# Threshold attention followed by a SwiGLU block: a slot's closing steps issued behind the next slot's masks, a chunk's last sigmoids issued with its last value product, and the first queries loaded in two parts

## The chip, the cores and the metric

The kernel runs on one core of one Trainium2 chip, in one launch. The metric is the device time in microseconds, and the median of several runs stands for it. Before the change three runs took 1599.44, 1601.48 and 1604.86 us, so the median is 1601.48 us. One profiled execution took 1599.08 us; its span, from the first to the last instruction, is 1597.3 us, and all times inside the profile count from the start of that span.

The engines are named as in the profile: PE is TensorE's matrix multiplication and PEld its loading of weights, DVE is VectorE, ACT is ScalarE, POOL is GpSimd, and SP is SyncE, which here only issues transfers. Each engine works through its own queue of instructions in order.

## The reference

Attention over 8 batches and 8 heads, 576 queries and keys, head size 64. A probability counts only where its score comes within `tau` of the largest of its row. The result is then the input of a SwiGLU block with 512 inputs and 1536 hidden columns. Everything is float32.

```python
def _attn_ref(q, k, v, tau):                      # q, k, v: (8, 8, 576, 64), tau = 0.02
    scores = scale * np.matmul(q, k.transpose(0, 1, 3, 2))      # scale = 1 / sqrt(64)
    thresh = np.max(scores, axis=-1, keepdims=True) - tau
    scores = np.where(scores >= thresh, scores, -1000000000.0)
    scores = scores - np.max(scores, axis=-1, keepdims=True)
    attn = np.exp(scores)
    attn = attn / (np.sum(attn, axis=-1, keepdims=True) + 1e-09)
    return np.matmul(attn, v).astype(np.float32)

def _moe_ref(x, w_gate, w_val, w_out):            # x: (4608, 512), d_ff = 1536
    g = x @ w_gate
    silu = g * (1.0 / (1.0 + np.exp(-g)))
    val = x @ w_val
    return (silu * val @ w_out).astype(np.float32)
```

The weights come as float64 and are put together into float32 by the kernel (splitting on ScalarE, joining on VectorE and GpSimd), which takes up the first 225 us or so.

## The kernel before

The work is cut into **segments**: one segment is two heads of one batch. A segment has **slots**, each of which makes the scores of up to 2 x 128 queries. Eight segments of a first kind (`halved` is false) come first; 28 segments of five slots each follow (`halved` is true), and most of the span is theirs. Between the slots, pieces of the SwiGLU block are given to TensorE: `fill(part)` issues such pieces until `part` is used up. A **chunk** (or unit) is 256 rows of the SwiGLU block.

A slot's `scores` is a generator. What stands before each `yield` is issued together, and the loop further down decides what comes in between.

```python
def scores(seg, t):
    ...                                    # scores on TensorE into two PSUM tiles "sc" (a pool of 2)
    if halved:
        for x, tile_ in enumerate(pss):    # L315: maximum of each half row, VectorE
            nc.vector.tensor_reduce(out=mx[:, 2 * x:2 * x + 2, 0], in_=tile_[:, :, 0:SH], axis=AX.X, op=ALU.max, negate=True)
        meet(mx, m, largest)               # L271: halves of a row exchanged between partitions, VectorE
        nc.vector.tensor_reduce(out=nm[:, 0:m], in_=mx[:, 0:m, :], axis=AX.X, op=ALU.min)            # L318
    ...
        nc.scalar.activation(th[:, 0:m], nm[:, 0:m], AF.Identity, bias=cut, scale=-1.0)              # L327 (L330)
    for x in range(m):
        nc.scalar.activation(ps[x], scs[x], AF.Exp, bias=nm[:, x:x + 1])                             # L331
    yield                                                                                            # first
    turn(1)                                # L365: transposes p of earlier slots, VectorE; keeps the last 1
    for x in range(m):                     # L335: the masks; they also sum each half row
        nc.vector.scalar_tensor_tensor(out=ps[x], in0=scs[x], scalar=th[:, x:x + 1], in1=ps[x],
                                       op0=ALU.is_ge, op1=ALU.mult, accum_out=sm[:, x, 0:1])
    tot = stp.tile([P, 4], F32, name="tot")
    if halved:
        yield                                                                                        # second
        meet(sm, m, same)                  # L274: partial sums exchanged, four small copies on ScalarE
        yield                                                                                        # third
        nc.vector.tensor_reduce(out=tot[:, 0:m], in_=sm[:, 0:m, :], axis=AX.X, op=ALU.add)           # L342
    ...
    nc.vector.reciprocal(out=ri[:, 0:m], in_=tot[:, 0:m])                                            # L345
    ...
    for x in range(m):
        if halved and not split and x % 2:
            nc.gpsimd.tensor_scalar(out=ps[x], in0=ps[x], scalar1=ri[:, x:x + 1], ...)               # L350
        else:
            nc.scalar.activation(ps[x], ps[x], AF.Copy, scale=ri[:, x:x + 1])                        # L352
    if halved:
        unturned.append([seg["p"][:, x, :] for x in at])
    ...
    yield                                                                                            # fourth
```

The loop over the slots, cut to the order of issue:

```python
for n, seg in enumerate(segs):
    for x, t in enumerate(seg["tiles"]):
        go = scores(seg, t)
        next(go)                       # scores, maximum, threshold, exponential
        ...                            # value products p v of the segment before, in its second slot (L432)
        split_weights(); ...
        next(go)                       # transposes of an earlier slot, masks
        if more:
            join_weights()
        fill(part)                     # SwiGLU pieces
        next(go)                       # exchange of the sums
        if len(unsig) >= SIG:
            sigmoids()
        fill(part)                     # SwiGLU pieces
        next(go)                       # sum, reciprocal, scaling
        ...
```

The pieces of a chunk: `gate` (L475, matrix 0) ends with a copy of the product by ScalarE (L491), `value` (L475, matrix 1) ends with a multiplication by VectorE (L498), `sigmoids` puts the sigmoid on what has gathered (ScalarE, L509) and multiplies it in (GpSimd, L511), then loads the exponential's table again (L514). The output of most chunks is computed by seven products of half the size in place of eight (`seven`, L584), for which `sigmoids` also makes sums on GpSimd (L522 to L524). `output` (L551) is the plain form, for the first two chunks.

```python
def sigmoids():
    eng = nc.vector if attended else nc.gpsimd
    for hts, gt, own in unsig:
        nc.scalar.activation(gt, gt, AF.Sigmoid)
        for y, (x, ht) in enumerate(own):
            eng.tensor_tensor(out=ht, in0=ht, in1=gt[:, 2 * y:2 * y + 2, :], op=ALU.mult)
    ...

def block():                           # the SwiGLU pieces in order; fill() takes them one by one
    ...
        for f in range(0, NF, GR):
            if f == EARLY:
                yield from late        # outputs of the chunk before
            yield from gate(j, cs, f, hts, gts)
            ...
            yield from value(j, cs, f, hts, gts)
            if not ready and f == NF - 2 * GR:
                sigmoids()
        if unsig:
            sigmoids()
        late = outputs(unit)
```

The start: `load_qk(0)` fetches q (SyncE's queue) and k (ScalarE's queue) in four transfers each, scales q by 0.125 (L241 on ScalarE for the first two segments, L243 on GpSimd afterwards), and `prepare` transposes k, the first 256 columns of q and the other 320 (L759 to L761).

Of the kernel before, what the change touches and what calls it, by code (L numbers as in the profile page):

```python
# [19 lines left out]
def kernel(  # L20
# [202 lines left out]
    def load_qk(i):  # L223
        b, hp_ = divmod(i, NP)
        raws = []

        free = {1: 0, 2: 1}.get(i)
        for name, src, order in (("q", q, "(j r) (e d) -> e r j d"), ("k", k, "(j r) (e d) -> e r j d" if b == 0 else "(r j) (e d) -> e r j d")):
            if free is None:
                raw = ld.tile([P, NJ, G], F32, name=f"{name}raw")  # L230
            else:
                n = 2 * free + len(raws)
                raw = extra[:, n * S:(n + 1) * S].rearrange("p (j d) -> p j d", d=G)
            queue = nc.scalar if i < 2 and name == "k" else nc.sync
            for g in range(NG):
                h, e = divmod(g, 2)
                queue.dma_start(out=raw[g * G:(g + 1) * G],
                                  in_=src[b, 2 * hp_ + h].rearrange(order, r=G, d=G)[e])
            raws.append(raw.rearrange("p j d -> p (j d)"))
        if i < 2:  # L240
            nc.scalar.activation(raws[0], raws[0], AF.Copy, scale=scl)  # L241
        else:
            nc.gpsimd.tensor_scalar(out=raws[0], in0=raws[0], scalar1=scl, scalar2=None, op0=ALU.mult)  # L243
        return raws

    def load_v(seg):
# [29 lines left out]
    def scores(seg, t):  # L276
        qT, kT, tiles, halved = seg["qT"], seg["kT"], seg["tiles"], seg["halved"]
        if halved and "p" not in seg:
            seg["p"] = arenas[seg["i"] % 2]
        q0 = t * P - seg["q0"]  # L280
        heads = [slice(h * D, (h + 1) * D) for h in range(2)]
        if t < NT:
            pss = [ps_s.tile([P, 2, 512], F32, name="sc") for _ in range(2)]
            at = [t, NT + 1 + t]
        else:
            pss = [ps_s.tile([P, 2, 512], F32, name="sc")]
            at = [t]
        if halved:
            put = [(pss[u], h, q0 + u * D) for u in range(len(pss)) for h in range(2)]
            for x in range(0, len(put), 2):  # L290
                for g in range(NG):
                    a, c = divmod(g, 2)
                    for ps, h, col in put[x:x + 2]:
                        hs = heads[h]
                        nc.tensor.matmul(ps[g * G:(g + 1) * G, h, 0:SH], qT[hs, col + a * G:col + (a + 1) * G],  # L295
                                         kT[hs, c * SH:(c + 1) * SH], start=True, stop=True)
        elif t < NT:
            for h, hs in enumerate(heads):
                for n in range(2):
                    nc.tensor.matmul(pss[h][:, n, 0:SH], qT[hs, q0:q0 + P], kT[hs, n * SH:(n + 1) * SH],  # L300
                                     start=True, stop=True)
        else:
            for n, h in ((0, 0), (1, 1), (1, 0), (0, 1)):
                hs = heads[h]
                nc.tensor.matmul(pss[0][hs, n, 0:SH], qT[hs, q0:q0 + D], kT[hs, n * SH:(n + 1) * SH],
                                 start=True, stop=True)
        mx, nm, th, ri = (stp.tile([P, 4, 2] if x == "mx" else [P, 4], F32, name=x) for x in ("mx", "nm", "th", "ri"))
        sm = sums[0]
        sums.rotate(1)
        if halved:  # L310
            m = 2 * len(at)
            scs = [ps[:, h, 0:SH] for ps in pss for h in range(2)]
            ps = [seg["p"][:, x, u * SH:(u + 1) * SH] for u in range(2) for x in at]
            for x, tile_ in enumerate(pss):
                nc.vector.tensor_reduce(out=mx[:, 2 * x:2 * x + 2, 0], in_=tile_[:, :, 0:SH], axis=AX.X, op=ALU.max,  # L315
                                        negate=True)
            meet(mx, m, largest)
            nc.vector.tensor_reduce(out=nm[:, 0:m], in_=mx[:, 0:m, :], axis=AX.X, op=ALU.min)  # L318
        else:
            m = len(at)  # L320
            scs = [ps[:, :, 0:SH] for ps in pss]
            ps = [pbufs[0][:, x, :].rearrange("p (n s) -> p n s", n=2) for x in range(m)]
            pbufs.rotate(1)
            for x in range(m):
                nc.vector.tensor_reduce(out=nm[:, x:x + 1], in_=scs[x], axis=AX.XY, op=ALU.max, negate=True)
        if halved:
            nc.scalar.activation(th[:, 0:m], nm[:, 0:m], AF.Identity, bias=cut, scale=-1.0)  # L327
        for x in range(m):
            if not halved:
                nc.scalar.activation(th[:, x:x + 1], nm[:, x:x + 1], AF.Identity, bias=cut, scale=-1.0)  # L330
            nc.scalar.activation(ps[x], scs[x], AF.Exp, bias=nm[:, x:x + 1])  # L331
        yield
        turn(1)
        for x in range(m):
            nc.vector.scalar_tensor_tensor(out=ps[x], in0=scs[x], scalar=th[:, x:x + 1], in1=ps[x],  # L335
                                           op0=ALU.is_ge, op1=ALU.mult, accum_out=sm[:, x, 0:1])
        tot = stp.tile([P, 4], F32, name="tot")
        if halved:
            yield
            meet(sm, m, same)  # L340
            yield
            nc.vector.tensor_reduce(out=tot[:, 0:m], in_=sm[:, 0:m, :], axis=AX.X, op=ALU.add)  # L342
        else:
            nc.vector.tensor_reduce(out=tot[:, 0:m], in_=sm[:, 0:m, 0:3:2], axis=AX.X, op=ALU.add)
        nc.vector.reciprocal(out=ri[:, 0:m], in_=tot[:, 0:m])  # L345
        if not halved:
            yield
        for x in range(m):
            if halved and not split and x % 2:
                nc.gpsimd.tensor_scalar(out=ps[x], in0=ps[x], scalar1=ri[:, x:x + 1], scalar2=None, op0=ALU.mult)  # L350
# [5 lines that stand above are left out]
            unflipped.append((seg, t, [p.rearrange("p n s -> p (n s)") for p in ps]))  # L356
            yield
        yield
# [3 lines left out]
    def turn(keep):  # L362
        while len(unturned) > keep:
            for p in unturned.popleft():
                nc.vector.transpose(out=p, in_=p)  # L365
# [128 lines left out]
    def value(j, cs, f, hts, gts):  # L494
        n = cs.stop - cs.start
        per = rows_per(n)
        ps = yield from rows_of_products(j, cs, f, 1, "pv")
        nc.vector.tensor_tensor(out=hts[f // 2][:, :, 0:n], in0=gts[f // per][:, f % per:f % per + GR, :], in1=ps,  # L498
                                op=ALU.mult)
        if f % per == per - GR:  # L500
            unsig.append((hts, gts.pop(f // per), [(x, hts[x][:, :, 0:n]) for x in range((f + GR - per) // 2, f // 2 + 1)]))
        if f == NF - GR and cs.stop == TC:
            del xts[j]
        yield HCOST

    def sigmoids():
        eng = nc.vector if attended else nc.gpsimd
        for hts, gt, own in unsig:
            nc.scalar.activation(gt, gt, AF.Sigmoid)  # L509
# [134 lines left out]
    def block():  # L644
        late, last = iter(()), None
        while True:
# [11 lines left out]
            for f in range(0, NF, GR):  # L658
                if f == EARLY:
                    yield from late  # L660
                yield from gate(j, cs, f, hts, gts)
                if f >= EARLY:
                    next(sums, 0)
                yield from value(j, cs, f, hts, gts)
                if not ready and f == NF - 2 * GR:

                    sigmoids()
            if unsig:
                sigmoids()
            late = outputs(unit)  # L670
            last = unit

# [74 lines left out]
    def prepare(seg):  # L747
# [8 lines left out]
        if i < NP:  # L756
# [1 line left out]
            rest = flat[:, i * (S - QA):(i + 1) * (S - QA)]  # L758
            nc.vector.transpose(out=kT, in_=kr)  # L759
            nc.vector.transpose(out=qT[:, 0:QA], in_=qr[:, 0:QA])  # L760
            nc.vector.transpose(out=rest, in_=qr[:, QA:S])  # L761
            kept[i] = {"kT": kT, "qT": rest, "q0": QA}
        else:
            kT = qkp.tile([P, S], F32, name="kT")
# [13 lines left out]
    fetch_weights(2)  # L778
    load_v(segs[0])
    fetch_weights(2)  # L780
    prev = None
    for n, seg in enumerate(segs):
        if NP <= n < 2 * NP:
            seg["v"] = segs[seg["i"]]["v"]
        for x, t in enumerate(seg["tiles"]):
# [21 lines left out]
            if x == 0 and n >= NP:  # L807
                fetch_qk(seg["i"] + 1)
            next(go)
            if more:  # L810
                join_weights()
            fill(part)
# [1 line left out]
            if len(unsig) >= SIG:  # L814
                sigmoids()
            fill(part)
            next(go)
            if attends and n > 2 * NP:
                next(products)
                next(products)  # L820
# [5 lines left out]
            if x == len(seg["tiles"]) - 2 and n + 1 < len(segs):  # L826
                prepare(segs[n + 1])
                if n < NP:
                    fetch_qk(segs[n + 1]["i"] + 1)
        prev = seg  # L830
    turn(0)
    fill(left[0])
    products = attend(prev)
# [37 lines left out]
```

## Time and profile before

| what | number |
|---|---|
| median time | 1601.48 us |
| span of the profiled execution | 1597.3 us |
| mean granted TensorE clock | 0.981 |
| TensorE busy | 1503.7 us |
| VectorE busy | 1046.9 us |
| ScalarE busy | 845.3 us |
| GpSimd busy | 660.7 us |
| mean DMA rate | 42 GB/s |

How to read it. The busy table counts the time in which an engine has an instruction at work. Matrix multiplications overlap, so a busy TensorE need not be one at its peak. A row of the waits reads "who waited, at which line, for whom at which line: total us, times, longest us". A row of the timeline reads "start, length, engine, line, operation, output <- input, how many merged", and in square brackets the idle time ahead of it with the engine that ended it. A row by stretches of time gives the busy time and, in brackets, the number of instructions of PE, PEld, DVE, ACT and POOL, then the granted TensorE clock as a part of full speed, the DMA engines' busy share and their rate.

### The profile page before, as it was taken

The page shows a single profiled execution, that of the slowest core. Times are in us where ns is not written, and L with a number is a line of the kernel's source. Part 1 is how long each engine was busy: PE and PEld are TensorE (multiplying, and loading weights), DVE is VectorE, ACT ScalarE, POOL GpSimd, SP SyncE. Part 2 cuts the span into 40 slices and gives each one's busy share as a digit, 9 for nine tenths or more (in the row PEclk, how much of TensorE's full clock was granted, in tenths as well). Part 3 has the DMA queues.
Part 4 walks back from the last instruction along what each step waited for, and adds up shares of the span by engine and source line. Part 5 has one row for each costly group of instructions (what it writes and reads, how often), then busy time and mean ns, then how long its engine had stood idle before and what let it go on. Part 6 is the DMA issues. An engine that isn't in the chain of part 4 may idle for free. (4 is left out here: it accounts for less than half of the span.)

```text
span 1597.3 us, 31341 instructions
## 1 busy us (share of the span) xinstructions
PE 1503.7 (94%) x11728; PEld 1131.2 (71%) x11728; DVE 1046.9 (66%) x3193; ACT 845.3 (53%) x2153; POOL 660.7 (41%) x650
## 2 busy tenths in 40 slices
PE   6899778899999999899999999999999999899998
PEld 3566555357776777678777777777777777688887
DVE  6888886877776767674767777767676777412212
ACT  5878756545565655545465655464647464511110
POOL 2545534327536353534363545344446354500011
PEclk9999899999999999999999999999999999999999
DMA  8541221111111111110211111101111120000000
GB/s 173 131 152 65 70 50 31 44 44 31 31 44 44 31 31 44 31 44 1 45 31 44 31 44 31 44 11 36 28 44 31 44 46 14 1 14 0 14 14 14
DMA packets 176423, 66.91 MB, mean 42 GB/s; under 512 B 159632, under 2 KB 159632, under 8 KB 176272
## 3 DMA queue, kind: packets, MB, share of 16 engines
q1 hardware_dynamic: 168592, 54.88, 15.6%
q0 software_dynamic: 2944, 9.44, 1.7%
q8 instruction: 93, 1.52, 0.4%
q10 hardware_dynamic: 4736, 0.59, 0.3%
q14 instruction: 58, 0.48, 0.1%
HBM read 55.44 MB, written 9.44 MB: 41 GB/s over the span
## 5 line engine op out<-in xcount | busy, mean ns | idle before, releaser
L475 PE MATMUL pg<-xall,wgv 128*128 128x256 f32 x1728 | 404.6, 386 | 0.5 <-DVE xall L412 0.5
L475 PE MATMUL pv<-xall,wgv 128*128 128x256 f32 x1728 | 401.5, 383 | 1.9 <-ACT gt L491 1.9
L475 PEld LDWEIGHTS pg<-xall,wgv 128*128 128x128 f32 x1728 | 326.6, 192 | 69.5 <-issue 19.0
L475 PEld LDWEIGHTS pv<-xall,wgv 128*128 128x128 f32 x1728 | 325.4, 191 | 66.8 <-issue 20.3
L350 POOL TENSOR_SCALAR pall<-pall,ri 128x288 f32<-128x288 f32 x243 | 241.7, 1005 | 273.5 <-DVE ri L345 238.9
L335 DVE SCALAR_TENSOR_TENSOR pall<-sc,th,pall 128x288 f32<-128x288 f32 (+1 forms) x540 | 258.1, 529 | 48.9 <-ACT pall L331 48.1
L331 ACT ACTIVATE pall<-sc,nm 128x288 f32<-128x288 f32 (+1 forms) x540 | 236.7, 510 | 0.4
L352 ACT ACTIVATE pall<-pall,ri 128x288 f32<-128x288 f32 (+1 forms) x297 | 152.7, 559 | 94.8 <-DVE ri L345 93.8
L295 PE MATMUL sc<-kT,qT 64*32 64x288 f32 x4032 | 161.8, 417 | 37.3 <-DVE pall L335 35.6
L315 DVE TENSOR_REDUCE mx<-sc 128x2 f32<-128x576 f32 x252 | 177.8, 743 | 23.3 <-PE sc L295 22.1
L365 DVE STREAM_TRANSPOSE pall<-pall 128x576 f32<-128x576 f32 x252 | 181.5, 754 | 7.1 <-POOL pall L350 7.1
L511 POOL TENSOR_TENSOR ht<-ht,gt 128x512 f32<-128x512 f32 x84 | 104.8, 1274 | 191.0 <-ACT gt L509 191.0
L274 ACT COPY sums<-sums 32x4 f32<-32x4 f32 (+1 forms) x560 | 108.5, 194 | 136.6 <-DVE pall L335 127.1
L584 PE MATMUL po<-wo,ht 128*128 128x256 f32 x768 | 180.1, 388 | 0.0
L584 PEld LDWEIGHTS po<-wo,ht 128*128 128x128 f32 x768 | 147.6, 194 | 29.2 <-issue 4.6
L498 DVE TENSOR_TENSOR ht<-gt,pv 128x512 f32<-128x512 f32 x102 | 69.9, 685 | 141.2 <-PE pv L475 118.1
L327 ACT ACTIVATE th<-nm,cut 128x4 f32<-128x4 f32 (+1 forms) x140 | 41.4, 295 | 215.3 <-DVE nm L318 215.3
L295 PEld LDWEIGHTS sc<-kT,qT 64*32 64x32 f32 x4032 | 58.9, 106 | 116.9 <-issue 83.5
L432 PE MATMUL xa<-pall,vall 64*64 64x288 f32 x2016 | 132.6, 410 | 9.2 <-issue 6.7
L432 PEld LDWEIGHTS xa<-pall,vall 64*64 64x64 f32 x2016 | 81.6, 135 | 56.3 <-issue 12.5
L597 POOL TENSOR_TENSOR ht<-ht,xall 128x256 f32<-128x256 f32 x48 | 35.0, 729 | 189.3 <-PE po L584 187.0
L491 ACT COPY gt<-pg 128x512 f32<-128x512 f32 x108 | 63.4, 587 | 79.0 <-PE pg L475 78.0
(106 smaller groups left out, 1493.0 us busy)
## 6 DMA issues: line engine op xcount, KB each, us to landing
vall<-in_v_dram SPq DMA_DIRECT2D x112, 144.0 KB, 3.3
qraw<-in_q_dram SPq DMA_DIRECT2D x120, 72.0 KB, 2.4
kraw<-in_k_dram SPq DMA_DIRECT2D x116, 72.0 KB, 2.8
out_dram<-ob POOLq DMA_DIRECT2D x32, 256.0 KB, 2.4
wo<-in_moe_w_gate_dram SPq DMA_DIRECT2D x16, 384.0 KB, 3.5
wo<-in_moe_w_val_dram SPq DMA_DIRECT2D x16, 384.0 KB, 4.1
xall<-in_moe_w_out_dram SPq DMA_DIRECT2D x6, 768.0 KB, 4.8
wo<-in_moe_w_out_dram SPq DMA_DIRECT2D x2, 768.0 KB, 4.7
```

The lines of the kernel that those rows point to most:

```text
L274: nc.scalar.copy(out, in_[:, :, 0])
L295: nc.tensor.matmul(ps[g * G:(g + 1) * G, h, 0:SH], qT[hs, col + a * G:col + (a + 1) * G], kT[hs, c * SH:(c + 1) * SH], start=True, stop=True)
L315: nc.vector.tensor_reduce(out=mx[:, 2 * x:2 * x + 2, 0], in_=tile_[:, :, 0:SH], axis=AX.X, op=ALU.max, negate=True)
L331: nc.scalar.activation(ps[x], scs[x], AF.Exp, bias=nm[:, x:x + 1])
L335: nc.vector.scalar_tensor_tensor(out=ps[x], in0=scs[x], scalar=th[:, x:x + 1], in1=ps[x], op0=ALU.is_ge, op1=ALU.mult, accum_out=sm[:, x, ...
L350: nc.gpsimd.tensor_scalar(out=ps[x], in0=ps[x], scalar1=ri[:, x:x + 1], scalar2=None, op0=ALU.mult)
L352: nc.scalar.activation(ps[x], ps[x], AF.Copy, scale=ri[:, x:x + 1])
L365: nc.vector.transpose(out=p, in_=p)
L432: nc.tensor.matmul(xa[a][h * D:(h + 1) * D, at:at + n * G].rearrange("d (i q) -> d i q", q=G), vr[rs, h, j, :], p[rs, lo:lo + n, j, :], st ...
L475: nc.tensor.matmul(ps[:, i], wgv[:, mat, c, (f + i) * P:(f + i + 1) * P], x[:, c, cs], start=(c == 0), stop=(c == NCC - 1))
L511: eng.tensor_tensor(out=ht, in0=ht, in1=gt[:, 2 * y:2 * y + 2, :], op=ALU.mult)
L584: nc.tensor.matmul(ps, h(f), w[:, f, :], start=(f == 0), stop=(f == NF2 - 1))
```

## The change

The change has three parts.

1. A slot's sum, reciprocal and scaling (everything after the third `yield`) are no longer issued at the end of the slot but in the next slot, right behind that slot's masks. The next slot's maximum and exponential no longer stand behind them in the queues of VectorE and ScalarE. Since the scaled p now comes a slot later into the list of what is to be transposed, `turn(0)` takes the place of `turn(1)`, and p is transposed in the same slot as before.
2. `sigmoids` for a chunk's end is issued inside `value`, ahead of its last `yield`, and so together with the last value product. Before, it was issued when the next piece was asked for, which can be after the next slot's exponential.
3. At the start, q of the first segment is fetched, scaled and transposed in two parts. The first 256 columns are what the first slots need; the other 320 are transposed with the second segment's. GpSimd, not ScalarE, scales q of the first two segments.

The diff, with blank lines left out:

```diff
@@ load_qk
-            for g in range(NG):
-                h, e = divmod(g, 2)
-                queue.dma_start(out=raw[g * G:(g + 1) * G],
-                                  in_=src[b, 2 * hp_ + h].rearrange(order, r=G, d=G)[e])
+            for js in [slice(0, QA // G), slice(QA // G, NJ)] if i == 0 and name == "q" else [slice(0, NJ)]:
+                for g in range(NG):
+                    h, e = divmod(g, 2)
+                    queue.dma_start(out=raw[g * G:(g + 1) * G, js],
+                                    in_=src[b, 2 * hp_ + h].rearrange(order, r=G, d=G)[e][:, js])
             raws.append(raw.rearrange("p j d -> p (j d)"))
-        if i < 2:
-            nc.scalar.activation(raws[0], raws[0], AF.Copy, scale=scl)
-        else:
-            nc.gpsimd.tensor_scalar(out=raws[0], in0=raws[0], scalar1=scl, scalar2=None, op0=ALU.mult)
+        for cs in [slice(0, QA), slice(QA, S)] if i == 0 else [slice(0, S)]:
+            nc.gpsimd.tensor_scalar(out=raws[0][:, cs], in0=raws[0][:, cs], scalar1=scl, scalar2=None, op0=ALU.mult)
@@ scores
         yield
-        turn(1)
+        turn(0)
@@ value
         if f == NF - GR and cs.stop == TC:
             del xts[j]
+        if f == NF - GR or f == NF - 2 * GR and not ready:
+            sigmoids()
         yield HCOST
     def sigmoids():
+        if not unsig:
+            return
         eng = nc.vector if attended else nc.gpsimd
@@ block
                 yield from value(j, cs, f, hts, gts)
-                if not ready and f == NF - 2 * GR:
-                    sigmoids()
-            if unsig:
-                sigmoids()
             late = outputs(unit)
@@ prepare
             nc.vector.transpose(out=qT[:, 0:QA], in_=qr[:, 0:QA])
-            nc.vector.transpose(out=rest, in_=qr[:, QA:S])
+            if i:
+                if i == 1:
+                    nc.vector.transpose(out=flat[:, 0:S - QA], in_=raws[0][0][:, QA:S])
+                nc.vector.transpose(out=rest, in_=qr[:, QA:S])
@@ the loop over the slots
-    prev = None
+    prev, last = None, iter(())
     ...
             next(go)
+            next(last, None)
             if more:
                 join_weights()
             fill(part)
     ...
             fill(part)
-            next(go)
+            last = go
     ...
         prev = seg
+    next(last, None)
     turn(0)
     fill(left[0])
```

## The prediction

> **What bounds the kernel now.** I read the page's busy table first, then the busy time by stage, then the waits of TensorE, and last the timeline around its longest gaps. From the page, and from the stage table (columns: stretch, length, then busy us and instructions of PE, PEld, DVE, ACT, POOL, the granted clock, DMA share, GB/s):
>
> ```profile
> PE 1503.7 (94%) x11728; PEld 1131.2 (71%) x11728; DVE 1046.9 (66%) x3193; ACT 845.3 (53%) x2153; POOL 660.7 (41%) x650
> ```
>
> ```profile
> 160.00:360.00 200.00, 165.28 (x1383) 101.95 (x1377) 155.04 (x483) 119.11 (x321) 78.88 (x65) 0.92 0.21 48
> 360.00:1400.00 1040.00, 1013.10 (x8470) 769.44 (x8463) 721.08 (x2354) 580.14 (x1569) 493.74 (x516) 0.99 0.15 33
> ```
>
> TensorE sets the time: 94% of the span. The change takes no matmul away, so all it can give back is TensorE's idle time, 1597.3 - 1503.7 = 93.6 us, and the time in which its clock is halved. The idle time is uneven: 26.4 us in the 160 us of the opening, 34.7 us in the 200 us in which the tiled slots begin and little feed-forward work is yet to be had, 26.9 us in the next 1040 us, 5.2 us at the end. The waits of TensorE (total, times, longest), over the whole span:
>
> ```profile
> PE sc L295 <- DVE pall L335: 35.6, 18, 5.7
> PE po L584 <- POOL ht L511: 15.1, 3, 6.5
> PE sc L300 <- DVE qT L760: 10.5, 1, 10.5
> PE sc L300 <- DVE pall L335: 9.1, 5, 2.7
> DVE tot L342 <- ACT sums L274: 60.5, 81, 4.3
> ```
>
> The first row is the main one: the next slot's scores wait until the masks (L335) have emptied the score buffers. The second is a chunk's output products waiting for its last sigmoids. The third is the start. The last row is no wait of TensorE, but it is what the change removes: VectorE stands before the sum of p (L342) until ScalarE has copied the partial sums across partitions (L274), and the next slot's maximum (L315) stands behind it in VectorE's queue. One such case, by engine, around the gap that ends at 587.31:
>
> ```profile
> 577.05 1.28 ACT L509 ACT_TABLE_LOAD   x1
> 581.56 0.84 ACT L274 COPY sums<-sums 32x2 f32<-32x2 f32 x4
> 582.43 0.16 DVE L342 TENSOR_REDUCE tot<-sums 128x2 f32<-128x6 f32 x1 [4.31 <-ACT sums L274]
> 582.70 1.40 DVE L315 TENSOR_REDUCE mx<-sc 128x2 f32<-128x576 f32 x2
> 587.31 0.72 PE L295 MATMUL sc<-kT,qT 64*32 64x288 f32 x16 [2.87 <-DVE pall L335]
> ```
>
> Scores began at 577.86 and took 1.20 us, so the maximum could have run from 579.1. It ran at 582.70, because the four copies sat behind a sigmoid batch that ended at 581.5. From there the chain is fixed: maximum, threshold, exponential, masks, and TensorE waits 2.87 us.
>
> **What the Trainium skill says.** "TensorE: Matmul & The Clock Gate", What's actually happening: after an idle window of about 3.4 us the array runs at half clock, until it has been busy for as long. The trace agrees. After the 3.75 us gap that ends at 492.87, the clock over 493 to 500 is 0.78, which costs 0.22 x 7 = 1.5 us more:
>
> ```profile
> 492.87 2.07 PE L584 MATMUL po<-extra,ht 128*128 128x256 f32 x4 [3.75 <-POOL ht L511]
> 493.00:500.00 7.00, 7.00 (x52) 5.14 (x53) 1.73 (x5) 1.93 (x7) 5.12 (x7) 0.78 0.34 85
> ```
>
> "ScalarE: Activation LUTs", What ACT_TABLE_LOAD costs: about 1283 ns for each load, whatever the set. The trace has 1.28 us, and a sigmoid batch pays it twice (to the sigmoid's set and back), which is why a batch holds ScalarE for 3.4 to 4.5 us. "Trainium Kernel Development and Optimization", Key Constraints: DMAs issued from the SP and ACT queues run on the same 16 engines and save only issue time. So I expect k's arrival not to move when q is split.
>
> **Part 1, the closing steps behind the next masks.** No work is added or removed. Per slot VectorE's sum (0.16) and reciprocal (0.18) leave the place ahead of the maximum, and with them goes the wait for ScalarE's copies. ScalarE's scaling (2 x 0.5 us) also leaves the place ahead of the next exponential. What it is worth, gap by gap, in 160 to 360:
> - gap at 193.11 (5.68 us): the maximum began at 188.51, VectorE was free and the scores there at 186.2. 2.3 us.
> - gap at 283.83 (4.15 us): maximum at 279.24, scores done at 276.9. 2.3 us, and the clock dip after it (0.76 over 7 us, 1.7 us) should go.
> - gap at 264.59 (2.54 us, value products waiting for transposes): the sum before it waited 3.72 us; scores were done at 258.4, the maximum ran at 261.55. The whole gap, 2.5 us.
> - gap at 243.59 (3.53 us): here the exponential is late, behind a sigmoid batch and 0.94 us of scaling. 0.9 us.
> - gaps at 172.66, 209.92 and 221.83: VectorE is busy without a break with joining the weights. Only the 0.34 us of sum and reciprocal each, 1 us.
> - 318.86, 326.20, 331.85 (1.80, 0.64, 2.15 us): of 4.6 us I take 2, and 1.7 us for one clock dip (0.76 over 331 to 338).
> Sum 11.0 + 3.4 = 14.4 us of the 34.7. From 360 to 1400 the row of the scores has 10.8 us in 8 waits. The one at 587.31 goes whole: 3.6 us of advance against 2.87, plus the clock (0.76 over 587 to 594, 1.7 us) = 4.6. Of the other 7.9 us I take half, 4. Together 8.6.
>
> **Part 2, the sigmoids with the last value product.** At 492.87 and 668.83 the order was: last value product's multiplication on VectorE at 484.12 (660.20), sigmoid only behind the next slot's exponential at 490.85 (666.81), GpSimd's multiplication behind it, TensorE at last. Issued with the product, the sigmoid can run some 5 us earlier:
>
> ```profile
> 484.12 0.68 DVE L498 TENSOR_TENSOR ht<-gt,pv 128x512 f32<-128x512 f32 x1
> 489.55 1.28 ACT L509 ACT_TABLE_LOAD   x1
> 491.56 1.26 POOL L511 TENSOR_TENSOR ht<-ht,gt 128x512 f32<-128x512 f32 x1 [1.97 <-ACT gt L509]
> ```
>
> Both gaps go: 3.75 + 1.5, and 4.88 + 2.3 (clock 0.62 over 669 to 675). That is 12.4 us. The third, 6.49 us at 1391.52, lies behind the last transposes, which wait for scalings behind a GpSimd batch. The batch gets earlier by half a slot, so 2 us. Sum 14.4.
>
> **Part 3, the start.** The first score waits 10.49 us: k is transposed at 7.55 for 0.78 us, the whole of q is scaled by ScalarE at 9.18, and 256 of its columns are transposed at 9.99. With 256 columns first, scaled by GpSimd (1.73 us for 576 columns elsewhere in this trace, so about 0.8), q is no longer last. k is, and the first score can start near 8.8, 1.7 us sooner. Against it: the table load of 1.28 us, until now ahead of q's scaling, will stand behind the wait of the first threshold. And 0.47 us of transposing the other 320 columns moves between slots 0 and 1. Net 0.5 us.
>
> **What is added.** ScalarE now waits after an exponential until the masks and the reciprocal of the slot before are done, and the copies of gates (L491) queue behind that. Example: masks end at 938.70, the scaling would run to 940.0, and copies that could go at 937.6 come at 940. VectorE's multiplications wait for them, ahead of the next maximum. Four PSUM buffers hide most of this. I put 20 slots at 0.4 us, 8 us. GpSimd's scaling now has some 3 us until its transposes instead of a slot. VectorE's wait for it is 7.1 us in 3 cases, and I add 2 us on TensorE's path. Sum 10.
>
> **Sum:** 14.4 + 8.6 + 14.4 + 0.5 - 10 = 27.9 us off. From the 1601.5 us of the median that is 1573.6. As gap by gap sums lean to the hopeful side, I say 1575.
>
> **Rivals.** (a) *The new wait takes the gain.* ScalarE blocks on masks, gate copies come late, and VectorE's wait for gates (18.4 us now) grows to far more. For it: in the steady stage masks end only 0.3 us before the next scores start (938.70 and 939.02), so there is little slack. Against: a gate's copy has four buffers of 3.3 us each before TensorE stops. It would leave about 1590 to 1600. (b) *GpSimd becomes the step that ends last.* A sigmoid batch with the sums for the seven products holds it for 10.6 us (406.8 to 417.4), scalings come behind, and transposes wait. It would make 1585 to 1595. (c) *The full gain.* All 35.6 us of score waits and two output waits with their clock dips go: about 1555 to 1562. Against it: in three gaps VectorE is simply full. (d) *Transfers hide nothing*: DMA is at 0.21 of its time in the stage concerned, so no transfer takes over there.
>
> **Range and chances.** The gain has two well-founded pieces, the two sigmoid gaps and the gap at 587, together 17 us, and softer ones. So a slowdown is unlikely. Faster by over 2% needs under 1569.5, 5.5 us below my figure: 0.35. Within 2%: 0.62. Slower: 0.03. Eight in ten: 1561 to 1593.
>
> **What would show it.** Right: VectorE's wait of L342 for sums falls from 60.5 us to under 10; score waits for L335 fall from 35.6 to 12 to 18; output waits for L511 go from three to one; the clock over 160 to 360 rises above 0.92; the first score starts before 9.5. Wrong: VectorE's wait of L498 for gates above 45 us, or of L365 for L350 above 20 us, with TensorE idle in 360 to 1400 no less than 26.9 us.

## The result and the profile after

The changed kernel takes 1607.39 us (median of four runs, 1604.0 to 1608.9) against 1601.48 us: a ratio of 1.0032, with a 95% interval from 1.0008 to 1.0055. It is 0.3% slower, where I had predicted 1575 us. The profiled execution spans 1601.9 us.

From the page of the changed kernel, and from its busy time by stretches (columns as before):

```profile
PE 1500.6 (94%) x11728; PEld 1125.6 (70%) x11728; DVE 1041.7 (65%) x3193; ACT 846.4 (53%) x2154; POOL 662.8 (41%) x653
```

```profile
160.00:360.00 200.00, 168.54 (x1436) 102.99 (x1436) 159.14 (x494) 120.61 (x329) 80.40 (x68) 0.94 0.23 52
360.00:1400.00 1040.00, 1001.70 (x8389) 758.64 (x8382) 709.84 (x2336) 580.26 (x1561) 486.81 (x511) 0.99 0.15 32
```

The stretch from 160 to 360 us is better: TensorE is idle 31.5 us there, not 34.7. The next 1040 us are worse: 38.3 us idle, not 26.9. The waits of TensorE and VectorE in the changed kernel show what stands behind that (line numbers have moved: L343 is the sum of p, L351 GpSimd's scaling, L353 ScalarE's scaling, L366 the transposes, L492 the gate copies, L499 the multiplications by them, L517 the sigmoid products):

```profile
PE sc L295 <- DVE pall L335: 34.4, 18, 4.5
PE sc L295 <- DVE tot L343: 16.1, 20, 3.0
PE po L590 <- POOL ht L517: 10.3, 3, 7.4
DVE tot L343 <- ACT sums L274: 1.8, 1, 1.8
DVE pall L335 <- ACT pall L331: 70.4, 54, 4.2
DVE ht L499 <- ACT gt L492: 49.4, 32, 3.3
DVE pall L366 <- POOL pall L351: 17.6, 8, 4.9
```

The wait that the change was to remove is gone: VectorE waits 1.8 us for the copied sums, not 60.5. Yet the next slot's scores wait longer than before, 50.5 us against 35.6. The 34.4 us are joined by 16.1 us put down to L343, and those are the same wait: the sum is now the instruction right behind the last mask, and the profile names what ended last (at 576.48 the scores go on 0.15 us after that mask's end at 576.33, as in the other gaps). Of VectorE's waits that have grown, the last three rows bear on the closing steps. In the kernel before, the rows for exponentials, gates and scalings were these:

```profile
DVE pall L335 <- ACT pall L331: 48.1, 44, 4.2
DVE ht L498 <- ACT gt L491: 18.4, 6, 3.9
DVE pall L365 <- POOL pall L350: 7.1, 3, 3.6
```

Two stretches of the changed kernel's timeline show how. First a gate copy held back by the scaling ahead of it on ScalarE:

```profile
400.26 0.96 ACT L353 ACTIVATE pall<-pall,ri 128x288 f32<-128x288 f32 x2 [1.32 <-DVE ri L346]
401.13 0.56 ACT L492 COPY gt<-pg 128x512 f32<-128x512 f32 x1
401.73 0.69 DVE L499 TENSOR_TENSOR ht<-gt,pv 128x512 f32<-128x512 f32 x1 [1.50 <-ACT gt L492]
402.33 1.41 DVE L315 TENSOR_REDUCE mx<-sc 128x2 f32<-128x576 f32 x2
```

ScalarE stands 1.32 us until the reciprocal, which stands behind the masks. Then it scales, and only then does it copy the gate, whose product had been done since about 395.5. VectorE waits 1.50 us for that copy, with the next maximum behind it. Second, the gap at 587 of the prediction, which was to vanish:

```profile
582.52 1.99 POOL L351 TENSOR_SCALAR pall<-pall,ri 128x288 f32<-128x288 f32 x2
584.53 0.78 DVE L366 STREAM_TRANSPOSE pall<-pall 128x576 f32<-128x576 f32 x1 [4.94 <-POOL pall L351]
586.31 2.18 PE L295 MATMUL sc<-kT,qT 64*32 64x288 f32 x32 [3.73 <-DVE pall L335]
```

GpSimd had a batch of sigmoid products, and then the sums for the seven products, until 582.5 and scaled only after them. The transposes, which stand ahead of the masks, waited 4.94 us for that, and TensorE waited 3.73 us, more than the 2.87 us before.

### The profile page after: what moved, and what is told of

It reads as the page before. It is cut to its first block, busy times and chain, and to the rows that moved or that the text cites. A ratio compares the mean times of both kernels' runs of the same rounds, so it can differ in the third digit from the quotient of the medians.

```text
span 1601.9 us, 31197 instructions
## 1 busy us (share of the span) xinstructions
PE 1500.6 (94%) x11728; PEld 1125.6 (70%) x11728; DVE 1041.7 (65%) x3193; ACT 846.4 (53%) x2154; POOL 662.8 (41%) x653
## 5 line engine op out<-in xcount | busy, mean ns | idle before, releaser
L351 POOL TENSOR_SCALAR pall<-pall,ri 128x288 f32<-128x288 f32 x243 | 241.7, 1005 | 548.9 <-DVE ri L346 516.7
L335 DVE SCALAR_TENSOR_TENSOR pall<-sc,th,pall 128x288 f32<-128x288 f32 (+1 forms) x540 | 258.5, 529 | 71.2 <-ACT pall L331 70.4
L353 ACT ACTIVATE pall<-pall,ri 128x288 f32<-128x288 f32 (+1 forms) x297 | 152.7, 559 | 213.3 <-DVE ri L346 213.2
L295 PE MATMUL sc<-kT,qT 64*32 64x288 f32 x4032 | 163.6, 419 | 50.8 <-DVE pall L335 34.4
L366 DVE STREAM_TRANSPOSE pall<-pall 128x576 f32<-128x576 f32 x252 | 182.3, 756 | 17.6 <-POOL pall L351 17.6
L499 DVE TENSOR_TENSOR ht<-gt,pv 128x512 f32<-128x512 f32 x102 | 68.9, 676 | 152.9 <-PE pv L476 100.0
L295 PEld LDWEIGHTS sc<-kT,qT 64*32 64x32 f32 x4032 | 58.8, 106 | 132.7 <-issue 99.0
L517 POOL TENSOR_TENSOR ht<-ht,gt 128x512 f32<-128x512 f32 x84 | 104.8, 1274 | 74.9 <-ACT gt L515 74.9
L433 PEld LDWEIGHTS xa<-pall,vall 64*64 64x64 f32 x2016 | 78.2, 134 | 57.9 <-DVE pall L366 8.2
L274 ACT COPY sums<-sums 32x4 f32<-32x4 f32 (+1 forms) x560 | 108.5, 194 | 11.2
L492 ACT COPY gt<-pg 128x512 f32<-128x512 f32 x108 | 62.3, 577 | 75.6 <-PE pg L476 74.6
L594 DVE TENSOR_TENSOR ob<-ob,po 128x256 f32<-128x256 f32 x96 | 38.5, 415 | 92.5 <-PE po L590 63.1
```

The lines of the kernel that those rows point to most:

```text
L274: nc.scalar.copy(out, in_[:, :, 0])
L433: nc.tensor.matmul(xa[a][h * D:(h + 1) * D, at:at + n * G].rearrange("d (i q) -> d i q", q=G), vr[rs, h, j, :], p[rs, lo:lo + n, j, :], st ...
```

## The experiments

All runs are compared with the kernel before, measured on the same chip beside them. Ratios are given with their 95% intervals. By these intervals a difference between two edited kernels is good to some 4 or 5 us.

### Each part alone, and the change without part 1

The edits are those of the diff above: part 1 only, part 2 only, part 3 only, and parts 2 and 3.

> Only part 1 (closing steps behind the next slot's masks) on the kernel before. Theory P (part 1 loses: scalings start 6 us later, so GpSimd's share is late for the transposes and ScalarE's holds back gate copies): slower, about 1608 us (+5 to +12), with VectorE waiting for L350's scalings over 15 us in total and for gate copies over 40 us. Rival Q (part 2 loses: a sigmoid batch now stands ahead of the next exponential, and part 1 is good by itself): faster, about 1594 us (-5 to -12).

> Only part 2 (sigmoids issued with a chunk's last value product) on the kernel before. Theory P: faster, about 1594 us (-5 to -12), because the two output waits of 3.75 and 4.88 us and their half-clock spells go. Rival Q: no gain or slower, 1600 to 1610 us, because VectorE waits longer for exponentials (over 60 us in place of 48) and each time scores come late.

> Only part 3 (first queries in two parts, scaled by GpSimd) on the kernel before. Both theories: 1.5 us faster, 1600 us, as the two traces stand 1.5 us apart from 30 us to 150 us in front of every part that could differ otherwise.

> Parts 2 and 3 without part 1. Theory P: the sum of both, about 1592 us (-7 to -13). Rival Q: 1598 to 1608 us.

| kernel | median us | ratio to before |
|---|---|---|
| part 1 alone | 1633.58 | 1.0201 (1.0179 to 1.0223) |
| part 2 alone | 1583.99 | 0.9889 (0.9870 to 0.9907) |
| part 3 alone | 1598.25 | 0.9987 (0.9976 to 0.9999) |
| parts 2 and 3 | 1579.93 | 0.9863 (0.9843 to 0.9882) |
| all three (the change) | 1607.39 | 1.0032 (1.0008 to 1.0055) |

Theory P holds, and more strongly than expected. Part 1 alone costs 32 us, and on top of parts 2 and 3 it costs 1607.39 - 1579.93 = 27.5 us. Part 2 brings 17 us, part 3 about 3, both more than I expected. My expectation for part 1 alone, 5 to 12 us, was too small; VectorE's waits for scalings (16.9 us) and for gates (71.6 us) passed the marks of theory P. By itself it also lengthens the output waits for sigmoid products. In the run with part 1 alone that row is

```profile
PE po L584 <- POOL ht L511: 26.7, 5, 9.2
```

against 15.1 us in three waits before. At two of the five (7.63 and 9.13 us) a chunk's last sigmoid stands on ScalarE behind the next slot's exponential and now also behind a scaling that waits for masks, while GpSimd waits for the sigmoid. At the first of them:

```profile
499.58 0.96 ACT L352 ACTIVATE pall<-pall,ri 128x288 f32<-128x288 f32 x2 [1.41 <-DVE ri L345]
500.56 1.28 ACT L509 ACT_TABLE_LOAD   x1
502.57 1.26 POOL L511 TENSOR_TENSOR ht<-ht,gt 128x512 f32<-128x512 f32 x1 [0.94 <-ACT gt L509]
```

Part 2 is not at fault: without part 1 it gives more than the 14.4 us of the prediction, and its output waits are down to one:

```profile
PE po L589 <- POOL ht L516: 4.8, 1, 4.8
```

Its exponentials do come later behind the sigmoid batches (VectorE waits 58.4 us for them, not 48.1), as the rival theory said, but without harm to the time.

### Closing steps ahead of the next masks instead of behind them

The same move into the next slot, but issued right behind the next slot's exponential, so that the sum waits for nothing. p gets into the list ahead of `turn`, so one entry is kept as in the kernel before:

```diff
             go = scores(seg, t)
             next(go)
+            next(last, None)
     ...
             next(go)
-            next(last, None)
             if more:
                 join_weights()
@@ scores
-        turn(0)
+        turn(1)
```

> Parts 2 and 3, and the closing steps issued in the next slot ahead of its masks (right behind its exponential, turn(1) as before) instead of behind them. Theory M (part 1 loses only because the sum now waits for the next masks, 3 to 5 us longer than needed): under the 1579.9 us of the kernel without part 1, about 1570 us, score waits for masks from 33 to under 22 us, waits of L342's kind for copied sums near 0. Rival N (moving the closing steps into the next slot costs in itself, since ScalarE's scalings come between the exponential and the gate copies): 1585 to 1600 us.

> As the run with the closing steps ahead of the masks, without part 2. Theory M: 1586 us, that is its gain of some 10 us stands by itself on the 1598 us of part 3 alone. Rival N: 1603 to 1620 us.

Measured: 1570.71 us with parts 2 and 3 (ratio 0.9799, 0.9777 to 0.9821), and 1586.45 us with part 3 alone (0.9900, 0.9880 to 0.9920). Theory M holds in both, and the first of these is the fastest kernel of the study, 2% under the kernel before. So the move into the next slot is good in itself, by 1579.93 - 1570.71 = 9.2 us (1598.25 - 1586.45 = 11.8 us without part 2). Its place behind the masks costs 1607.39 - 1570.71 = 36.7 us. VectorE's waits in the fastest kernel:

```profile
DVE mx L314 <- PE sc L294: 54.1, 49, 3.1
DVE pall L334 <- ACT pall L330: 36.3, 47, 4.2
DVE ht L497 <- ACT gt L490: 4.9, 5, 2.5
DVE tot L341 <- ACT sums L273: 2.9, 2, 2.1
```

Gates are no longer late (4.9 us), VectorE waits less for exponentials than without the move (36.3 us against 58.8), and hardly at all for the copied sums (2.9). One number of my expectation failed: score waits for masks fell only from 32.8 to 29.3 us, not under 22. VectorE waits 55.5 us less for sums (58.4 us without the move), but 34.5 us more for the scores themselves: the first row was 19.6 us without the move. Most of that idle time had thus been beside TensorE's work, not on its path.

### Which queue loses it

Three edits of the changed kernel. First, all scalings on ScalarE (the GpSimd branch of the scaling is left unused), then the closing steps one place later, behind the first SwiGLU pieces:

```diff
-            next(last, None)
             if more:
                 join_weights()
             fill(part)
+            next(last, None)
             next(go)
```

> The changed kernel with all scalings on ScalarE and none on GpSimd (243 more there, 0.5 us each). Theory G (part 1 loses on GpSimd's queue: its share stands waiting for the reciprocal and holds back sigmoid products and sums, and transposes wait for it): most of the loss comes back, 1582 to 1592 us. Rival S (part 1 loses on ScalarE's queue: gate copies behind the scalings): slower still, 1610 to 1625 us.

> The changed kernel with the closing steps issued one step later: behind the first SwiGLU pieces of the next slot instead of ahead of them, so that those pieces' gate copies and GpSimd work go first. Theory S: faster than the changed kernel, 1585 to 1598 us, waits for gate copies from 47 down to 20 us. Theory G: slower, 1612 to 1630 us, as GpSimd's share comes later still and waits of transposes for it pass 30 us.

> Closing steps behind the first pieces (as e7) and all scalings on ScalarE (as e6): gate copies go ahead of the scalings, and no transpose waits for GpSimd. If the two routes S (gate copies behind ScalarE's scalings) and G (GpSimd's late share) are the whole loss: 1583 to 1595 us. If part 1 loses by something else as well, such as late exponentials: 1603 us or more.

| edit of the changed kernel | median us | ratio to before | VectorE's wait for gates, us | its transposes' wait for GpSimd, us |
|---|---|---|---|---|
| none | 1607.39 | 1.0032 (1.0008 to 1.0055) | 49.4 | 17.6 |
| all scalings on ScalarE | 1622.01 | 1.0121 (1.0100 to 1.0142) | 81.0 | no such row |
| behind the first pieces | 1610.10 | 1.0047 (1.0030 to 1.0064) | 3.9 | 44.0 |
| both | 1586.70 | 0.9903 (0.9885 to 0.9922) | 5.0 | no such row |

Neither single-route theory holds. The first run fell into the range of theory S, the second into neither range: each of these two edits closes one route and opens the other further. With more scalings on ScalarE the gate copies come later still. With the gate copies first, GpSimd's scalings come later still:

```profile
DVE ht L497 <- ACT gt L490: 81.0, 35, 3.7
DVE pall L364 <- POOL pall L349: 44.0, 10, 8.5
```

(the first row is of the kernel with all scalings on ScalarE, the second of that with the closing steps behind the first pieces). Both edits together close both routes, and 20.7 of the 27.5 us come back, although VectorE then waits 107.1 us for exponentials, more than in any other run.

The last two edits close one route each and leave the other as it is. ScalarE's share goes to VectorE, straight behind the reciprocal, and the transposes go one slot later, except in a segment's second slot, where the value products of the segment before need them:

```diff
@@ scores (e10)
             if halved and not split and x % 2:
                 nc.gpsimd.tensor_scalar(...)
+            elif halved and not split:
+                nc.vector.tensor_scalar(out=ps[x], in0=ps[x], scalar1=ri[:, x:x + 1], scalar2=None, op0=ALU.mult)
             else:
                 nc.scalar.activation(...)
@@ scores (e11)
-        turn(0)
+        turn(1 if halved and seg["tiles"].index(t) != 1 else 0)
```

> The changed kernel with ScalarE's share of the scalings (where no weights are being split) on VectorE, straight behind the reciprocal; GpSimd keeps its share. ScalarE no longer waits for the reciprocal. Theory S: 1588 to 1597 us in place of 1607, VectorE's wait for gate copies back under 25 us, for exponentials under 60 us. Theory G: 1605 to 1615 us.

> The changed kernel with the transposes of a slot's p put off by one slot wherever the value products allow it, so that they no longer wait for GpSimd's scaling (17.6 us now). Theory G (this part of it): 1595 to 1601 us, VectorE's wait for scalings under 5 us. Theory S: 1604 to 1610 us.

> Both edits of e10 and e11. If S and the transposes' wait are the whole loss of 27 us: 1580 to 1586 us. If GpSimd's queue matters beyond the transposes (sigmoid products and output sums behind scalings that wait): 1588 to 1597 us.

Measured: 1587.54 us with the scalings on VectorE (0.9911, 0.9894 to 0.9927), 1596.20 us with later transposes (0.9968, 0.9957 to 0.9980), and 1577.26 us with both (0.9852, 0.9830 to 0.9874), a little under the expected range. Closing ScalarE's route brings 19.9 us, closing the transposes' route 11.2 us, and both together 30.1 us, about the sum. That is as much as part 1 costs; the interval overlaps that of the kernel without part 1. Of the kernel with both:

```profile
DVE ht L499 <- ACT gt L492: 4.9, 2, 2.5
DVE pall L366 <- POOL pall L349: 2.7, 3, 1.9
PE po L590 <- POOL ht L517: 2.6, 1, 2.6
```

TensorE's idle time between 360 and 1400 us moves with it: 38.3 us in the changed kernel, 21.5 us with the scalings on VectorE, 28.7 us with later transposes, 13.7 us with both, and 15.8 us without part 1. The rows of the last two, in this order:

```profile
360.00:1400.00 1040.00, 1026.26 (x8614) 782.73 (x8613) 811.57 (x2572) 486.63 (x1369) 510.04 (x519) 1.00 0.15 33
360.00:1400.00 1040.00, 1024.17 (x8586) 778.75 (x8585) 720.68 (x2353) 582.55 (x1575) 491.12 (x517) 1.00 0.15 33
```

In the kernel with the scalings on VectorE, the 19.9 us come although VectorE gets 113 us more to do:

```profile
L351 DVE TENSOR_SCALAR pall<-pall,ri 128x288 f32<-128x288 f32 x243 | 113.1, 503 | 4.8
```

This edit frees ScalarE as a whole, so the 19.9 us are for gate copies and for exponentials behind them together (VectorE's wait for exponentials falls from 70.4 to 41.2 us). How they divide was not tried.

Nor was either of these edits tried on the kernel without part 1, so a part of the 19.9 and 11.2 us may be a gain that they bring by themselves. VectorE's transposes wait for GpSimd there too: 11.0 us without part 1 and 14.1 us in the fastest kernel, against 17.6 us in the changed one. What speaks for the two routes is the pair tried first: all scalings on ScalarE and the later place lose time one by one, and together they bring back 20.7 us.

## Why the prediction was wrong, step by step

- **What bounds the kernel, and the chain at 587:** right. TensorE's idle time is what moved, and the maximum did stand behind the copied sums. Two small readings were off: the idle time at the end is 5.5 us, not 5.2, and ahead of the gap at 209.92 VectorE was not joining weights without a break but had waited 1.06 us for a gate copy.
- **Part 1's gain, 14.4 + 8.6 = 23 us:** wrong in size. In the kernel where the move stands undisturbed (closing steps ahead of the masks) it is 9.2 us. The step that failed is reading an advance of the maximum as an advance of TensorE gap by gap: with the move TensorE's idle time fell by 3.0 us between 160 and 360 and by 1.2 us between 360 and 1400, where the prediction counted 11.0 and 6.9. At 587 the 3.6 us of advance met GpSimd's backlog instead: even in that best kernel the same slot has a gap of 2.93 us, after transposes that waited 3.68 us for scalings.
- **What is added, 10 us:** this is the step that decided the result. The place behind the masks, against that ahead of them, measured 36.7 us. Both routes were named, and both were sized too small. Against the 8 us of "20 slots at 0.4 us" for the gate copies stand 19.9 us by the edit that closes that route, and against the 2 us for the transposes 11.2 us; neither figure is certain to be the route's cost alone. The buffers that I set against the first route hold TensorE's products; they do not help VectorE, which takes the multiplication and the next maximum in order. Rival (a) and rival (b) came true together, and the time lies above the ranges of both. A slowdown had been called unlikely because two pieces of the gain, 17 us together, were well-founded: the sigmoids' piece came, that at 587 did not, and the added waits outran the rest.
- **Part 2, 14.4 us:** right, and a little low: it measured 17 us alone. The two output waits and their half-clock spells went, as in the prediction; in the changed kernel as it is, 1.47 us of each wait stayed, and the clock behind them was 1.00. The third output wait, which was to shrink by 2 us, grew from 6.49 to 7.37 us with part 1 in place and is 4.8 us without it.
- **Part 3, 0.5 us:** too small, about 3 us by the medians and 2.4 us in the trace of that kernel. The step that failed is the table load behind the first threshold's wait. In the changed kernel it runs ahead of that wait, beside TensorE (lines below). This 1.28 us, and the 0.5 us by which the first score came ahead of 8.8 us, make up nearly all of the difference. k's arrival, which was not to move, came earlier: its transposition began at 6.73 to 7.20 us in the eleven kernels with q in two parts, and at 7.46 to 7.55 us in the three without. What moved it was not tried.

```profile
7.82 0.40 DVE L761 STREAM_TRANSPOSE qT<-qraw 128x256 f32<-128x256 f32 x1
8.21 1.28 ACT L330 ACT_TABLE_LOAD   x1 [8.21 <-DMA extra<-in_k_dram]
8.27 2.30 PE L300 MATMUL sc<-pall,qT 64*128 64x288 f32 x8 [8.27 <-DVE qT L761]
11.39 0.30 ACT L330 ACTIVATE th<-nm,cut 128x1 f32<-128x1 f32 x1 [1.90 <-DVE nm L325]
```

- **The signs to look for:** the sums' wait under 10 us, the first score before 9.5 us and a clock above 0.92 between 160 and 360 (0.94) came true. Score waits of 12 to 18 us did not, and the output waits stayed three, though they fell from 15.1 to 10.3 us. The signs of failure were set at 45 us for gates and 20 us for scalings. The first was passed (49.4), the second nearly (17.6), and the idle time from 360 to 1400 passed its mark by 11.4 us.

## What to carry to other kernels

An instruction moved later in a queue takes its own waits with it: before moving one out of the way, ask what it will wait for at the new place, and what then stands behind it on every engine it uses. Here the same steps, moved into the next slot ahead of its masks, gained 9 us, and a few instructions further, behind the masks, they lost 27. An engine's wait that vanishes is worth only what TensorE was waiting for; here 55 us less of waiting for sums on VectorE were 9 us of run time.

## What the runs showed of the hardware that I had not expected

The first table load of ScalarE did not stand behind the wait of the activation it serves: it ran at 8.21 us, and the activation waited until 11.39 us. A sigmoid batch's load, by contrast, started only when its data were ready (at 1392.72 us in the changed kernel, 0.07 us behind the multiplication it waits for). Which of the two a load does was not tried. VectorE scaled 128x288 elements in 0.50 us, where GpSimd took 1.005 us.

TensorE's half-clock spells did not need a gap as long as the 3.4 us that the prediction cites. In the kernel before they followed gaps of 2.15 and 2.87 us too (clock 0.76 over 331 to 338 and over 587 to 594), while behind the gaps of 1.47 us in the changed kernel (490.30 and 666.88) the clock stayed at 1.00.
